# Loop projections in 64-row halves, and the feed-forward tiles turned by DMA, in a fused attention and routed-FFN kernel

## The chip, the cores and the metric

One core of one Trainium2 chip. The metric is the device time of one execution in microseconds. The kernel before takes 1410.74 us (median of three runs, 1410.70 to 1410.93).

## The reference

x is 2048 x 512 in float32. Two branches are mixed by a gate.

```python
# A: softmax attention, 32 heads of 16
qkv = (x @ wqkv).reshape(B, S, 3, 32, 16)
p = softmax(einsum("bhqd,bhkd->bhqk", q, k) * 16 ** -0.5)
a = einsum("bhqk,bhkd->bhqd", p, v) ... @ wo
# B: two tokens of 2048 are routed through a SwiGLU FFN of width 1792
r = x @ w_r
idx = argsort(-r)[:2]
y = (silu(x[idx] @ w_gate) * (x[idx] @ w_up)) @ w_down
b = x; b[idx] += y * sigmoid(r[idx])
g = sigmoid((x * gate_w).sum(-1))
out = g * a + (1 - g) * b
```

## The kernel before

**Work.** Heads are taken in pairs, each pair in two halves of 1024 queries: 32 units. A unit has 16 steps, one for each 128 keys, so there are 512 steps. A step makes S^T for two heads and two blocks of 512 queries: four S^T pieces (`s_piece`, L668), each one 50-row product into a `st` tile of PSUM and one exp on ACT into a quarter of the `P` tile of that step (L671, L677). A row of the 50 carries the negated row maximum, so that the exp needs no subtraction. The maxima of a unit are made 21 steps ahead: 64 pieces a unit (`m_piece`, L584), each one 48-row product, and DVE takes the maximum straight out of PSUM (L598): two pieces together from `mxa`, one from `mxb`. When a unit's pieces are done, `m_unit` (L644) reduces them on DVE and splits the result on POOL in two (L77, L78); `m_rows` transposes it and SP writes it into rows 48 and 49 of `Qx`. `p_v` (L940, product at L698) multiplies the `P` tile of a step with V: four column blocks of 32, accumulated over the unit in `av`.

**Two heads, two row halves.** The two heads of a pair lie in rows 0 to 63 and 64 to 127 of `Qx` and `Kx`. Pieces of S^T and of the maxima use either half (j = 0 or 1), and two that follow one another in different halves run side by side in the array. P·V, the projections and the output products use all 128 rows.

**Buffers.** PSUM has eight banks: three for `st`, two for `mxa`, one each for `mxb`, `av` and `fl`. `P` has three buffers in SBUF, `o` six, `w` (weights and later small tiles) three. The program order is written out by hand; each engine runs its own instructions in that order, and waits come from the tiles.

**The main loop** (L1000) is a string, ORDER (L31). One pass is a slot: 12 S^T pieces (s), 12 pieces for the maxima (m), three P·V (A) and one filling step (f). 164 slots cover all the maxima. At a slot's start `run_late` issues what was put off (evictions of `fl`, mostly). `at_step` hangs other work on step numbers, `gaps` hangs small DVE work behind a reduction.

**What fills.** `slots` (L882) is a generator that f advances; a yield ends a slot's share. It runs the projections of q and k for the groups 1 to 3 (`proj`, L147: 12 products of 128 rows into `fl`, three a slot, 24 projections; `evict`, L204: one copy on ACT, two instructions on POOL, stores by SP), then turns the two routed rows of x (`x_rows`), then gate and up of the FFN (`ff_in`), their transposes (`ff_t`), the down product, the sum of its four column blocks (`ff_sum`), and then the output products with wo (`wo_groups`, `wo_last`).

**The end.** The last 20 steps have no maxima left (L1025): each takes two pairs of S^T pieces and one P·V, and every second one a filling step. Then `tail` (L800) finishes the last unit.

Of the kernel before, what the change touches and what calls it, by code (L numbers as in the profile page):

```python
# [23 lines left out]
LEAD = 21  # L24
# [6 lines left out]
ORDER = "sssmmA smssmmA msssmmf smssmmAm".replace(" ", "")  # L31
# [5 lines left out]
def gated_mix(ctx: ExitStack, tc: tile.TileContext, xT, x, wqkv, wo, w_rg, w_gate, w_up, w_down,  # L37
# [60 lines left out]
    rsel = cp.tile([2, 1], F32, name="rsel")  # L98
# [5 lines left out]
    x_scr = dram.tile([S, D], F32, name="x_scr")  # L104
    i_scr = dram.tile([128, 1], U32, name="i_scr")
# [40 lines left out]

    def proj(g, which, nb, piece):  # L147
        i = "qk".index(which)
        wh, wl = W[g]
        ps = fl_tile() if g else st_tile()  # L150
        n = 0
        for terms in (((wh, xh), (wl, xh)), ((wh, xl),)):
            for c in range(4):
                for a, b in terms:
                    nc.tensor.matmul(ps, a[:, i, c, :], b[nb][:, c, :], start=n == 0, stop=n == 11)  # L155
# [194 lines left out]
    def route_rows():  # L350

        nc.vector.max_index(idx8, top8, rg["row"])
        nc.gpsimd.tensor_copy(num8, idx8)
# [41 lines left out]
    def load_down(j):  # L395
        t = xp.tile([FK, 4, D], F32, tag=f"xh{j}", name=f"wd{j}")
        nc.sync.dma_start(t, ap(w_down, j * FC * D, [[D, FK], [FK * D, 4], [1, D]]))
        ff.setdefault("down", []).append(t)

    def ff_in(name):  # L400
# [7 lines left out]
        late.append((ff_evict, (name, [128, FC], ps)))  # L408
        yield

    def ff_evict(name, shape, ps):
        ff[name] = o_tile(name, shape)
        nc.scalar.activation(ff[name], ps, AF.Copy)

    def ff_t(i, name):
        ps = fl_tile((FK, 4, 128))
        for cc in range(4):
            nc.tensor.transpose(ps[:, cc, :], ff[name][:, cc * FK:(cc + 1) * FK], ident)
        late.append((ff_gu, (i, ps)))

    def ff_gu(i, ps):
        if i == 0:
            ff["gu"] = o_tile("gu", [FK, 2, 4, 4, 2])
        nc.scalar.activation(ff["gu"][:, i], ps.rearrange("p c (j m) -> p c j m", m=32)[:, :, :, 0:2], AF.Copy)

    def ff_act():
        ff["e"] = o_tile("ffe", [FK, 4, 4, 2])
        nc.scalar.activation(ff["e"], ff["gu"][:, 0], AF.Exp, scale=-1.0)
        ff["hT"] = o_tile("ffhT", [FK, 4, 4, 32])
        nc.gpsimd.memset(ff["hT"], 0.0)  # L430
        nc.gpsimd.tensor_scalar(ff["e"], ff["e"], 1.0, None, op0=OP.add)
        nc.gpsimd.tensor_mul(ff["gu"][:, 1], ff["gu"][:, 0], ff["gu"][:, 1])

    def ff_h():
        nc.vector.reciprocal(ff["e"], ff["e"])
        nc.gpsimd.tensor_mul(ff["hT"][:, :, :, 0:2], ff["gu"][:, 1], ff["e"])

    def ff_down():
        ps = fl_tile()
        for cc in range(4):  # L440
            for j in range(4):
                nc.tensor.matmul(ps[32 * j:32 * j + 32, :], ff["hT"][:, cc, j, :], ff["down"][j][:, cc, :],  # L442
# [3 lines left out]
        late.append((ff_evict, ("y4", [128, D], ps)))  # L446
        yield

    def ff_sum():
        ps = fl_tile((2, 512))  # L450
        nc.tensor.matmul(ps, sel_j, ff["y4"], start=True, stop=True)
        late.append((ff_out, (ps,)))

    def ff_out(ps):
        y = o_tile("ffy", [2, D])
        nc.scalar.activation(y, ps, AF.Copy, scale=rsel[:, 0:1])
        nc.gpsimd.tensor_add(y, y, xsel)
        nc.gpsimd.indirect_dma_start(out=x_scr, out_offset=bass.IndirectOffsetOnAxis(ap=idx2[:, :1], axis=0),
                                     in_=y, in_offset=None)
# [5 lines left out]
    acc = []  # L465
# [10 lines left out]
    def acc_add(t, ps, scale):  # L476
# [3 lines left out]
        nc.gpsimd.tensor_add(a, a, w)  # L480
# [3 lines left out]
    def load_wo():  # L484
        s = ring.tile([128, 4, D], F32, tag="xs", name="wos", bufs=2)
        nc.sync.dma_start(s, ap(wo, 0, [[D, 128], [128 * D, 4], [1, D]]))
# [24 lines left out]
    def wo_terms(ps, ah, al, c, sl, first, last):  # L511
        for n, (a, b) in enumerate(((ah, wop[0]), (al, wop[0]), (ah, wop[1]))):
            nc.tensor.matmul(ps, a[:, sl], b[:a.shape[0], c, :], start=first and n == 0, stop=last and n == 2)  # L513
# [55 lines left out]
    def wo_last(t, k):  # L569
# [4 lines left out]
        if now[0] < STEPS - LEAD - 1:  # L574
            late.append((acc_add, (t, ps, gg)))
        else:
            finish(t, ps)
        if k == 128:
# [288 lines left out]
    at_step(26, gather)  # L867
    at_step(-8, load_w, 1)
# [13 lines left out]
    def slots():  # L882
        for w, nb in order:
            yield from proj(1, w, nb, 3)
        late.append((split_w, (2,)))
        at_step(now[0] + 4, load_w, 3)
        x_rows()
        yield
# [11 lines left out]
        ff_t(0, "gate")  # L900
        yield
        yield from ff_in("up")
        ff_t(1, "up")
        late.append((ff_act, ()))
        at_step(now[0] + 3, gaps.append, ff_h)
        at_step(now[0] + 3, load_wo)
        for c in range(4):
            at_step(now[0] + 6 + c, split_wo, c)
        at_step(now[0] + 5, load_at, 0, (0, 1))
        at_step(now[0] + 13, split_at, 0, (0, 1))  # L910
        yield
        yield
        yield from ff_down()
        ff_sum()
# [4 lines left out]
        for t in range(16):  # L919
            at_step(s + 6 + t, acc_scale, t)  # L920
        yield
# [18 lines left out]
    def p_v(s):  # L940
# [10 lines left out]
        elif u == QU - 1:  # L951
            for i in range(8):
                at_step(s + 6 + i, gaps.append, partial(l_out, 3, i))
            for i in range(4):
                at_step(s + 16 + 2 * i, l_last, i // 2, i % 2)
                at_step(s + 19 + 2 * i, n_last, i // 2, i % 2)
            at_step(s + 27, split_last, 3)
# [41 lines left out]

    while count["m"] < UNITS * EL:  # L1000
# [3 lines left out]
        for o in ORDER:  # L1004
            if o == "s":
# [3 lines left out]
                s_piece(s, i % 2, i // 2)  # L1009
# [3 lines left out]
            elif o == "m":  # L1013
# [21 lines left out]
    end_step(STEPS + 2)  # L1035
# [36 lines left out]
```

## Time and profile before

| | |
|---|---|
| median of three runs | 1410.74 us |
| the profiled execution | 1410.52 us |
| its span in the trace | 1408.4 us |
| granted TensorE clock | 0.999 |
| instructions in the trace | 24050 |
| DMA | 101.24 MB, 72 GB/s over the span |

A row of the timeline is: start in us from the span's start, length in us, engine, line, operation, what is written and read, shape, count of merged instructions, and in brackets the idle time of the engine before it and what ended it. A row of groups ends with: busy us, mean ns of one, idle us before them. A row of windows is: stretch, its length, busy us (and count) of PE, PEld (weight loads), DVE, ACT, POOL, then granted clock, DMA share, GB/s. Ends of PE's products are modelled; its starts are measured. POOL's spans are rough.

### The profile page before, as it was taken

The page shows a single profiled execution, that of the slowest core. Times are in us where ns is not written, and L with a number is a line of the kernel's source. Part 1 is how long each engine was busy: PE and PEld are TensorE (multiplying, and loading weights), DVE is VectorE, ACT ScalarE, POOL GpSimd, SP SyncE. Part 2 cuts the span into 40 slices and gives each one's busy share as a digit, 9 for nine tenths or more (in the row PEclk, how much of TensorE's full clock was granted, in tenths as well). Part 3 has the DMA queues.
Part 4 walks back from the last instruction along what each step waited for, and adds up shares of the span by engine and source line. Part 5 has one row for each costly group of instructions (what it writes and reads, how often), then busy time and mean ns, then how long its engine had stood idle before and what let it go on. Part 6 is the DMA issues. An engine that isn't in the chain of part 4 may idle for free.

```text
span 1408.4 us, 24050 instructions
## 1 busy us (share of the span) xinstructions
PE 1401.3 (99%) x9093; PEld 626.8 (45%) x9093; DVE 1289.1 (92%) x1544; ACT 1169.6 (83%) x2262; POOL 318.0 (23%) x336
## 2 busy tenths in 40 slices
PE   9999999999999999999999999999999999999998
PEld 6754444444444444444444443444444444444433
DVE  6889999999999999999999999999999999999953
ACT  5578888888888888888888888888888888888987
POOL 3841101002000001200000100043822322233421
PEclk9999999999999999999999999999999999999999
DMA  8721201313132221312222342424312121111002
GB/s 260 280 50 39 55 30 39 84 39 77 38 81 94 70 61 46 77 39 74 63 91 61 94 107 70 103 60 121 84 46 54 32 61 35 30 31 46 18 28 105
DMA packets 54775, 101.24 MB, mean 72 GB/s; under 512 B 13168, under 2 KB 20592, under 8 KB 53028
## 3 DMA queue, kind: packets, MB, share of 16 engines
q1 hardware_dynamic: 53796, 98.62, 24.6%
q8 instruction: 72, 1.18, 0.4%
q10 hardware_dynamic: 576, 0.79, 0.2%
q0 software_dynamic: 288, 0.30, 0.1%
q14 instruction: 43, 0.35, 0.1%
HBM read 63.77 MB, written 36.96 MB: 72 GB/s over the span
## 4 chain that ended last, share of the span: by engine, by line
PE 99%; DVE 0%; DMA 0%; ACT 0%; issue 0%; DVEq 0%
PE av L698 36%; PE st L675 24%; PE mxa L594 12%; PE mxb L594 10%; PE fl L155 6%; PE fl L513 4%; PE st L301 3%; PE st L155 2%; PE fl L404 1%; PE mxa L628 0%; PE mxa L675 0%; PE fl L442 0%; DMA ws<-wqkv 0%; PE st L628 0%; PE av L301 0%; PE mxb L628 0%
## 5 line engine op out<-in xcount | busy, mean ns | idle before, releaser
L677 ACT ACTIVATE P<-st 128x512 f32<-128x512 f32 x2009 | 1055.0, 599 | 186.5 <-PE st L675 97.7
L598 DVE TENSOR_REDUCE Mr<-mxa 128x2 f32<-128x1024 f32 x655 | 796.3, 1216 | 1.5 <-PE mxa L594 1.3
L698 PE MATMUL av<-P,V 128*32 128x512 f32 x4096 | 545.5, 605 | 0.2 <-DVE o L710 0.2
L675 PE MATMUL st<-Qx,Kx 50*128 50x512 f32 x2009 | 530.8, 443 | 0.2 <-ACT P L677 0.2
L598 DVE TENSOR_REDUCE Mr<-mxb 128x1 f32<-128x512 f32 x654 | 451.2, 690 | 59.7 <-PE st L675 18.8
L675 PEld LDWEIGHTS st<-Qx,Kx 50*128 50x128 f32 x2009 | 277.0, 184 | 227.0 <-ACT P L677 209.0
L594 PE MATMUL mxb<-Kx,Qx 48*128 48x512 f32 x654 | 325.2, 497 | 0.0
L594 PE MATMUL mxa<-Kx,Qx 48*128 48x512 f32 x1310 | 293.7, 417 | 0.0
L594 PEld LDWEIGHTS mxb<-Kx,Qx 48*128 48x128 f32 x654 | 119.5, 183 | 273.7 <-DVE Mr L598 272.5
L698 PEld LDWEIGHTS av<-P,V 128*32 128x32 f32 x4096 | 81.1, 108 | 142.1 <-issue 135.3
L594 PEld LDWEIGHTS mxa<-Kx,Qx 48*128 48x128 f32 x1310 | 123.1, 183 | 44.4 <-DVE Mr L598 2.3
L208 POOL TENSOR_SCALAR ev<-pe 128x512 fp32r<-128x512 f32 x24 | 35.8, 1490 | 411.4 <-ACT pe L206 411.4
L480 POOL TENSOR_TENSOR acc<-acc,w 128x512 f32<-128x512 f32 x37 | 47.3, 1281 | 200.5 <-ACT w L479 200.5
L77 POOL TENSOR_SCALAR hl<-m 128x16 fp32r<-128x16 f32 x31 | 7.8, 252 | 296.4 <-DVE m L646 296.4
L155 PE MATMUL fl<-xh,wh 128*128 128x512 f32 x96 | 42.9, 447 | 0.0
L155 PE MATMUL fl<-xh,wl 128*128 128x512 f32 x96 | 40.4, 421 | 0.0
L513 PE MATMUL fl<-woh,ahl 128*128 128x512 f32 x96 | 35.2, 447 | 0.0
L564 DVE SCALAR_TENSOR_TENSOR acc<-fl,gg,acc 128x512 f32<-128x512 f32 x11 | 8.2, 747 | 29.1 <-PE fl L513 29.1
L155 PE MATMUL fl<-xl,wh 128*128 128x512 f32 x96 | 32.6, 421 | 0.0
L209 POOL TENSOR_TENSOR ev<-pe,ev 128x512 fp32r<-128x512 f32 x24 | 30.9, 1286 | 2.0
L303 ACT ACTIVATE V<-st 128x512 f32<-128x512 f32 x15 | 9.0, 598 | 23.7 <-PE st L301 23.7
L474 POOL TENSOR_SCALAR acc<-acc,omg 128x512 f32<-128x512 f32 x16 | 24.8, 1565 | 10.5 <-DMA acc<-x_scr 10.5
(189 smaller groups left out, 789.2 us busy)
## 6 DMA issues: line engine op xcount, KB each, us to landing
Kx<-k_scr SPq DMA_DIRECT2D x30, 384.0 KB
Qx<-q_scr SPq DMA_DIRECT2D x52, 192.0 KB
q_scr<-ev SPq DMA_DIRECT2D x15, 512.0 KB
k_scr<-ev SPq DMA_DIRECT2D x13, 512.0 KB
xn<-x SPq DMA_DIRECT2D x4, 1024.0 KB
Qx<-hr SPq DMA_DIRECT2D x256, 2.0 KB
acc<-x_scr SPq DMA_DIRECT2D x4, 1024.0 KB
q_scr<-ev SPq DMA_DIRECT2D x15, 256.0 KB
```

The lines of the kernel that those rows point to most:

```text
L155: nc.tensor.matmul(ps, a[:, i, c, :], b[nb][:, c, :], start=n == 0, stop=n == 11)
L208: nc.gpsimd.tensor_scalar(ev[:, 0], t, 1.0, None, op0=OP.mult)
L209: nc.gpsimd.tensor_sub(ev[:, 1], t, ev[:, 0].bitcast(F32))
L301: nc.tensor.matmul(ps, a[nb][:, c, sl], b[:, c, :], start=c == 0 and n == 0, stop=c == 3 and n == 2)
L474: nc.gpsimd.tensor_scalar(a, a, omg[:, t:t + 1], None, op0=OP.mult)
L480: nc.gpsimd.tensor_add(a, a, w)
L513: nc.tensor.matmul(ps, a[:, sl], b[:a.shape[0], c, :], start=first and n == 0, stop=last and n == 2)
L594: nc.tensor.matmul(dst, Qx[u % 3][64 * j:64 * j + 48, t * 128:t * 128 + 128], k_of(u, t // 4)[64 * j:64 * j + 48, c * 512:c * 512 + 512], ...
L598: nc.vector.tensor_reduce(Mr[:, g0:g0 + (2 if r == 1 else 1)], MX[r - 1], axis=AX.X, op=OP.max, negate=True)
L675: nc.tensor.matmul(ps, k, q, start=True, stop=True)
L677: nc.scalar.activation(P[s][:, 2 * j + c, :], ps, AF.Exp)
L698: nc.tensor.matmul(AV[0][32 * ct:32 * ct + 32, :], V[:, kt, h * VW:h * VW + 32], P[s][:, ct, :], start=kt == 0, stop=kt == KT - 1)
```

## The change

- In slots 1 to 95 the three products of a projection's slot become six of 64 rows: h for rows 0 to 63, H for rows 64 to 127, set among the pieces of S^T and of the maxima by a new ORDER, in which a capital is a piece or half in rows 64 to 127. A half that follows one of the other rows waits, through a nop on POOL, until that one has ended, since both add into one bank.
- Slot 0 and the slots from 96 on keep the old order, written as ORDER_FF.
- In the new ORDER the second P·V of a slot stands after nine S^T pieces; before, after six.
- The routed rows of x, and gate and up, are turned by DMA instead of transposes on PE; the four blocks of the down product are added on POOL instead of PE. This takes four filling slots out.
- The last 20 steps run three pairs of S^T pieces to a turn and then the P·V that are ready, with a filling step every second turn: six output products there, ten before.
- The weight splits of groups 2 and 3 are issued at the end of the projections of the group before; the scaling of `acc` is spread over more steps; `wo` is loaded in four transfers.

```diff
-ORDER = "sssmmA smssmmA msssmmf smssmmAm".replace(" ", "")
+ORDER = "sSsmMASmShMmhhSMsHHsHsmMAmSsSMmAM"
+ORDER_FF = "sSsmMA SmsSMmA MsSsmMf SmsSMmAM".replace(" ", "")
+H_SLOTS = range(1, 96)
...
+    pend, fresh, halving = [[], []], [], [False]
+    def mm(ps, a, b, start, stop):
+        if not halving[0]:
+            nc.tensor.matmul(ps, a, b, start=start, stop=stop)
+            return
+        if start:
+            fresh.append(ps)
+        for j in range(a.shape[0] // 64):
+            pend[j].append((ps, a[64 * j:64 * j + 64], b[64 * j:64 * j + 64]))
+        last_one[0] = stop
+    def half(j):
+        if pend[j]:
+            ps, a, b = pend[j].pop(0)
+            stop = not pend[0] and not pend[1] and last_one[0]
+            i = nc.tensor.matmul(ps, a, b, start=bool(fresh), stop=stop)
+            if before[0] is not None and before[1] != j:
+                n = nc.gpsimd.nop()
+                tc.add_manual_dep(n.ins, before[0].ins.name, SYNC, reason="one bank")
+                tc.add_manual_dep(i.ins, n.ins.name, SYNC, reason="one bank")
+            before[:] = i, j
+            fresh.clear()
...
-                    nc.tensor.matmul(ps, a[:, i, c, :], b[nb][:, c, :], start=n == 0, stop=n == 11)
+                    (mm if g else nc.tensor.matmul)(ps, a[:, i, c, :], b[nb][:, c, :], start=n == 0, stop=n == 11)
...
-            if (g, which, nb) == (2, "q", 3):
-                late.append((split_w, (3, (1,))))
-                at_step(now[0] + 2, split_w, 3, (0,))
+            if g < 3 and (which, nb) == ("q", 3):
+                late.append((split_w, (g + 1, (1,))))
+                at_step(now[0] + 3, split_w, g + 1, (0,))
...
     def x_rows():
-        ps = fl_tile((128, 4, 2))
-        for c in range(4):
-            nc.tensor.transpose(ps[:, c, :], xsel[:, c * 128:c * 128 + 128], ident[:2, :2])
-        late.append((nc.scalar.activation, (xselT[:, :, 0:2], ps, AF.Copy)))
+        nc.sync.dma_start(xs_scr, xsel)
+        for m in range(2):
+            nc.sync.dma_start(xselT[:, :, m], ap(xs_scr, m * D, [[1, 128], [128, 4]]))
+        for j in range(1, 4):
+            nc.sync.dma_start(rsel4[32 * j:32 * j + 2, :], rsel)
...
+    def ff_turn(name):
+        ff_evict(name, [128, FC], ff["ps"])
+        ff["T" + name] = o_tile("T" + name, [FK, 2, 16])
+        for m in range(2):
+            nc.sync.dma_start(ff["T" + name][:, m], ff[name].rearrange("(j m) n -> j m n", m=32)[:, m, :])
...
+    def ff_y4(ps):
+        ff_evict("y4", [128, D], ps)
+        yy = ring.tile([128, 2, D], F32, tag="w", name="yy", bufs=3)
+        ff["yy"] = yy[0:2, 0], yy[0:2, 1], o_tile("y3", [128, D])[0:2]
+        for j, t in enumerate(ff["yy"]):
+            nc.sync.dma_start(t, ff["y4"][32 * j + 32:32 * j + 34, :])
...
+    slot = 0
     while count["m"] < UNITS * EL:
         hold = count["A"] % KT == 0 and count["A"] > 0
         if not hold:
             run_late()
-        for o in ORDER:
+        whole = slot not in H_SLOTS
+        halving[0] = not whole
+        asked = False
+        for o in ORDER_FF if whole else ORDER:
+            j = int(o.isupper())
...
             else:
-                next(fills, None)
+                if not asked:
+                    asked = True
+                    next(fills, None)
+                if o in "hH":
+                    half(j)
+        slot += 1
-    for s in range(count["s"] // 4, STEPS + 2):
-        run_late()
-        if s < STEPS:
-            start_step(s)
-            s_pair(s, 0)
-            s_pair(s, 1)
-        p_v(s - 2)
-        if s < STEPS and (s - count["s"] // 4) % 2 == 0:
-            next(fills, None)
-        end_step(s)
+    first, done = count["s"] // 2, count["A"]
+    for k, p in enumerate(range(first, 2 * STEPS, 3)):
+        run_late()
+        for i in range(p, min(p + 3, 2 * STEPS)):
+            s, c = divmod(i, 2)
+            if c == 0:
+                start_step(s)
+            s_pair(s, c)
+            if c:
+                end_step(s)
+        ready = (p + 1) // 2
+        for s in range(done, ready):
+            p_v(s)
+            if s == done and k % 2 == 0:
+                next(fills, None)
+        done = ready
```

More of the change, by code (lines that the diff above doesn't have):

```diff
@@ L97, in gated_mix @@
     Mr = cp.tile([128, 3 * EL], F32, name="Mr")
-    rsel = cp.tile([2, 1], F32, name="rsel")
+    rsel4 = cp.tile([128, 1], F32, name="rsel")
+    rsel = rsel4[0:2, :]
     xsel = cp.tile([2, D], F32, name="xsel")
@@ L104, in gated_mix @@
     x_scr = dram.tile([S, D], F32, name="x_scr")
+    xs_scr = dram.tile([2, D], F32, name="xs_scr")
     i_scr = dram.tile([128, 1], U32, name="i_scr")
@@ L407, in ff_in @@
                 yield
-        late.append((ff_evict, (name, [128, FC], ps)))
+        ff["ps"] = ps
+        late.append((ff_turn, (name,)))
         yield
@@ L479, in acc_add @@
         nc.scalar.activation(w, ps, AF.Copy, scale=scale[:, t:t + 1])
-        nc.gpsimd.tensor_add(a, a, w)
+        if scaled.get(t, 0) > now[0]:
+            at_step(scaled[t], nc.gpsimd.tensor_add, a, a, w)
+        else:
+            nc.gpsimd.tensor_add(a, a, w)
     wop = []
@@ L485, in load_wo @@
         s = ring.tile([128, 4, D], F32, tag="xs", name="wos", bufs=2)
-        nc.sync.dma_start(s, ap(wo, 0, [[D, 128], [128 * D, 4], [1, D]]))
+        for c in range(4):
+            nc.sync.dma_start(s[:, c], ap(wo, c * 128 * D, [[D, 128], [1, D]]))
         wop.append(xp.tile([128, 4, D], F32R, tag="xl0", name="woh"))
@@ L512, in wo_terms @@
         for n, (a, b) in enumerate(((ah, wop[0]), (al, wop[0]), (ah, wop[1]))):
-            nc.tensor.matmul(ps, a[:, sl], b[:a.shape[0], c, :], start=first and n == 0, stop=last and n == 2)
+            mm(ps, a[:, sl], b[:a.shape[0], c, :], start=first and n == 0, stop=last and n == 2)
     def wo_part(t, gs):
@@ L867, in gated_mix @@
     at_step(26, gather)
+    at_step(36, x_rows)
     at_step(-8, load_w, 1)
@@ L953, in p_v @@
                 at_step(s + 6 + i, gaps.append, partial(l_out, 3, i))
[L954 to L957, printed above, removed]
+            for n, i in enumerate((3, 0, 1, 2)):
+                at_step(s + 15 + 2 * n, l_last, i // 2, i % 2)
+                at_step(s + 17 + 2 * n, n_last, i // 2, i % 2)
+            at_step(s + 18, split_last, 3)
         elif QU <= u < UNITS - 1:
```

103 lines of the change are left out of this document (50 added, 53 removed).

## The prediction

> **What bounds the kernel now.** I read the page first (engine shares, costliest groups), then the timeline of one stretch of the loop, slot by slot, then a slot with no filling work, then the windows of the end.
>
> ```profile
> span 1408.4 us, 24050 instructions
> PE 1401.3 (99%) x9093; PEld 626.8 (45%) x9093; DVE 1289.1 (92%) x1544; ACT 1169.6 (83%) x2262; POOL 318.0 (23%) x336
> ...
> L677 ACT ACTIVATE P<-st 128x512 f32<-128x512 f32 x2009 | 1055.0, 599 | 186.5 <-PE st L675 97.7
> L598 DVE TENSOR_REDUCE Mr<-mxa 128x2 f32<-128x1024 f32 x655 | 796.3, 1216 | 1.5 <-PE mxa L594 1.3
> L598 DVE TENSOR_REDUCE Mr<-mxb 128x1 f32<-128x512 f32 x654 | 451.2, 690 | 59.7 <-PE st L675 18.8
> ```
>
> PE is never idle by the page, yet DVE is 92% busy with two kinds of reduction, 1216 and 690 ns, and the two engines hand one buffer `mxa` and one buffer `mxb` to and fro. So I look at one passage of a slot (12 S^T pieces, 12 pieces for the maxima, three P·V, one filling burst `fl`).
>
> ```profile
> 300.31 0.46 PE L594 MATMUL mxa<-Kx,Qx 48*128 48x512 f32 x2
> ...
> 300.70 0.96 PE L155 MATMUL fl<-xl,wh 128*128 128x512 f32 x3
> ...
> 301.59 0.50 PE L594 MATMUL mxb<-Kx,Qx 48*128 48x512 f32 x1
> ...
> 302.17 0.51 PE L594 MATMUL mxa<-Kx,Qx 48*128 48x512 f32 x2
> ...
> 303.57 0.62 ACT L206 ACTIVATE pe<-fl 128x512 f32<-128x512 f32 x1
> 303.60 0.50 PE L594 MATMUL mxb<-Kx,Qx 48*128 48x512 f32 x1
> ...
> 304.17 0.40 PE L594 MATMUL mxa<-Kx,Qx 48*128 48x512 f32 x2
> 304.28 1.49 POOL L208 TENSOR_SCALAR ev<-pe 128x512 fp32r<-128x512 f32 x1 [20.66 <-ACT pe L206]
> ...
> 304.50 1.06 PE L698 MATMUL av<-P,V 128*32 128x512 f32 x8
> 304.74 1.22 DVE L598 TENSOR_REDUCE Mr<-mxa 128x2 f32<-128x1024 f32 x1
> 305.50 0.50 PE L594 MATMUL mxb<-Kx,Qx 48*128 48x512 f32 x1
> ...
> 305.83 0.46 PE L675 MATMUL st<-Qx,Kx 50*128 50x512 f32 x2
> 305.85 1.29 POOL L209 TENSOR_TENSOR ev<-pe,ev 128x512 fp32r<-128x512 f32 x1
> ...
> 306.08 0.45 PE L594 MATMUL mxa<-Kx,Qx 48*128 48x512 f32 x2
> ...
> 306.67 1.22 DVE L598 TENSOR_REDUCE Mr<-mxa 128x2 f32<-128x1024 f32 x1
> ...
> 308.37 0.50 PE L155 MATMUL fl<-xh,wh 128*128 128x512 f32 x1
> ```
>
> A slot is 7.67 us from burst to burst (300.70 to 308.37). Four `mxa` pairs divide it into four groups. With P·V in a group: pair at 304.17, P·V at 304.50, `mxb` at 305.50, next pair at 306.08, so 1.91. With the burst: 300.31 to 302.17, 1.86. Is the burst on the path? A slot that has none answers.
>
> ```profile
> 914.41 1.22 DVE L598 TENSOR_REDUCE Mr<-mxa 128x2 f32<-128x1024 f32 x1
> ...
> 922.15 1.22 DVE L598 TENSOR_REDUCE Mr<-mxa 128x2 f32<-128x1024 f32 x1
> ```
>
> ```profile
> 917.70 3.04 ACT L677 ACTIVATE P<-st 128x512 f32<-128x512 f32 x6 [0.33 <-PE st L675]
> 917.71 0.44 PE L594 MATMUL mxa<-Kx,Qx 48*128 48x512 f32 x2
> ...
> 918.28 1.22 DVE L598 TENSOR_REDUCE Mr<-mxa 128x2 f32<-128x1024 f32 x1
> ...
> 918.35 0.49 PE L675 MATMUL st<-Qx,Kx 50*128 50x512 f32 x1 [0.20 <-ACT P L677]
> ...
> 919.55 0.52 PE L594 MATMUL mxa<-Kx,Qx 48*128 48x512 f32 x2
> ...
> 920.12 1.23 DVE L598 TENSOR_REDUCE Mr<-mxa 128x2 f32<-128x1024 f32 x1
> ```
>
> Between these first and fifth `mxa` reductions no `fl` product runs, and the slot still takes 7.74. In its burstless group PE waits, for the exps (918.35) and then for the reduction of 918.28, which ends at 919.50 and lets the next pair go at 919.55. So three groups are as long as PE makes them with P·V, and the fourth is as long as DVE's turn of `mxa`. I take 7.70 for a slot.
>
> **The halves themselves.** In 95 slots three 128-row products become six of 64 rows. The burst holds PE from 300.70 to 301.59, 0.89; half a pair costs what a pair does, 0.25 (305.83 to 306.08). The new group without P·V is the one from the second `mxa` pair to the third: one half alone, half with S, M with s, one half alone, two halves with s, then the pair, 7 intervals, 1.75. I put time 0 at the slot's first `mxb` piece (303.60). Up to the second pair nothing of PE's order changes in kind: +2.48. PE alone would set the third pair at +4.23, but the reduction of 306.67 ends at 307.89, +4.29, so DVE sets it at +4.34, its second piece up to 0.1 later (in 919.55's pair: 0.52 for both, 0.40 for one). From there as now: P·V 0.33 later, `mxb` 1.00 on, fourth pair 0.58 on, next slot's `mxb` 1.33 on: +7.58 to +7.68. Alone the halves would be worth 7.63 - 7.70 = -0.07 a slot, -7 us for 95. Bounds: 0, and -21 if the burstless group fell to PE's own 1.75 and the others kept 1.91 (7.48 a slot).
>
> By the Trainium skill, page "TensorEngine Tiling (Array Packing)", Tiling Modes, "Changing tiling mode (not just tile) drains the TensorE"; the switches that this change takes out would then be worth up to the whole burst beyond three pairs. The burst row agrees that there is a price, the empty slot says that the slot does not pay it.
>
> **The moved P·V.** This I price highest. Now the second P·V of a slot follows the sixth S^T piece; in the new order it follows the ninth (count the s and S before the second A). The ninth opens a new step, so a fourth `P` tile, and `P` has 3 buffers, unchanged. The oldest is still to be read by that very P·V. So the ninth exp waits on ACT for the P·V behind it, and exps 10 to 12 queue behind it; `st` has 3 buffers too, so the twelfth S^T piece waits on PE for the ninth exp, and the fourth `mxa` pair, the last P·V and all else on PE stand behind that.
>
> ```profile
> 132.77 1.06 PE L698 MATMUL av<-P,V 128*32 128x512 f32 x8
> ...
> 133.90 0.60 ACT L716 ACTIVATE o<-av 128x512 f32<-128x512 f32 x1
> ```
>
> ACT goes 0.07 after the end of a P·V (133.83 to 133.90). P·V starts at +4.67 to +4.77, ends 1.06 later, the ninth exp runs from +5.80 to +5.90 for 0.60, the twelfth piece goes 0.05 after it (first of six exps 917.70 plus 0.60, PE at 918.35), at +6.45 to +6.55 in place of about +6.05. Fourth pair 0.25 later, next slot 1.33 after that: +8.03 to +8.13. I take 8.08: 0.38 over 7.70, 95 times, **+36 us**, the -7 in it. Bounds: 7.9 (the reduction starts as soon as in 919.55 to 920.12, and no late second piece) gives +19, 8.15 gives +43.
>
> **The relay through POOL.** Two halves of one bank are kept apart by a nop on POOL between h and H. The trace holds no nop. Its lower bound is the moment when POOL has handed out all that stands before it, its upper the end of that work; I take the lower plus 0.1, since the nop has nothing to compute and needs no result of POOL's. In an ordinary slot nothing stands before it: the third h goes at +2.98, lasts 0.40, and H at +3.48 is hardly held. But L208 and L209 (evict) and the splits of `hl` stand before it.
>
> ```profile
> L208 POOL TENSOR_SCALAR ev<-pe 128x512 fp32r<-128x512 f32 x23 | 34.3, 1490 | 392.8 <-ACT pe L206 392.8
> ...
> L77 POOL TENSOR_SCALAR hl<-m 128x16 fp32r<-128x16 f32 x18 | 4.5, 252 | 194.9 <-DVE m L646 194.9
> ```
>
> ```profile
> 198.06 0.47 PE L594 MATMUL mxa<-Kx,Qx 48*128 48x512 f32 x2
> ...
> 198.63 1.22 DVE L598 TENSOR_REDUCE Mr<-mxa 128x2 f32<-128x1024 f32 x1
> ...
> 200.52 0.22 POOL L78 TENSOR_TENSOR hl<-m,hl 128x16 fp32r<-128x16 f32 x1
> ```
>
> ```profile
> 159.26 0.45 PE L675 MATMUL st<-Qx,Kx 50*128 50x512 f32 x2
> ...
> 159.92 0.22 POOL L78 TENSOR_TENSOR hl<-m,hl 128x16 fp32r<-128x16 f32 x1
> ```
>
> Evict, 23 times: the first h is due with the S of 305.83; L209 is handed out at 305.85 when L208 is done: 0.1 each, 2.5. Unit ends, 18 in the loop's halved part, each third of them at another `mxa` pair of the slot (64 pieces a unit, 12 a slot). At the first pair: h due at 159.26, POOL past L78 at 159.92, so 0.75 late, six times, 4.5. At the second: H due four intervals after 198.06, 199.06; POOL past L78 at 200.52, so H at 200.6, the third pair 0.75 later at 201.37 where DVE allows 199.90: 1.45, six times, 8.7. At the third: the next half is a slot away, 0. The second part of the weight split now falls just before an H, twice: behind L209's end (307.14) one 1.49 op, H at 308.7 where 307.1 was due, 3. Early routing on POOL, 2: an estimate, four short waits for DVE or ACT of about one 0.5 step. Together **+21**. Bounds 0 and 54 (all POOL work to its end: 307.14 for 305.85, 23 times, and L78's 0.22).
>
> The Trainium skill, page "PSUM — Partial Sum Buffer", Engine vs sequencer instructions, says the sequencer only waits for prior instructions "to be *dispatched* to the engine, not to complete", which is the lower bound; by the other reading the sum would be 1498. No run here shows it yet.
>
> **FF by DMA, four slots less.** Removed: 12 transposes, the sum product, four ACT copies; added: some 13 small transfers on SP's queue, `wo` in four, a few POOL ops. PE's part was filling, and filling is free (7.74 empty, 7.67 full): 0. What hides it is DVE's turn of `mxa`; were that gone a burst would cost its 0.89. Each turned tile has a slot (7.7) until its first reader; On SP the reads of `xs_scr` wait for its write, and a turn waits for ACT's copy; behind them stand loads that are issued a unit ahead of their use. Bounds -2 and +3.
>
> **The end.**
>
> ```profile
> 1351.00:1397.00 46.00, 45.80 (x296) 15.40 (x297) 11.54 (x18) 41.89 (x72) 1.76 (x3) 1.00 0.17 59
> ```
>
> PE fills the 46 us, ACT 41.89 of them. Four bursts fewer and three pairs to a turn let ACT become the limit: at most -4, I take **-2**; +2 if a P·V comes to wait for its exps.
>
> **Sum.** The profiled execution took 1410.52 us with a span of 1408.4; the median of three runs is 1410.74. 1410.5 + 36 + 21 + 0 - 2 = 1465.5; I say **1465**.
>
> **Rivals.**
> (1) POOL relays only after its work has ended: 1465 + 33 = 1498. For it: h and H are PE's, the nop is in POOL's order. Against: it reads nothing of POOL's. 10%.
> (2) The ninth exp does not hold PE, some piece of slack covers it: 1465 - 43 = 1422. Against: `P` and `st` both have three buffers in the code, and the twelfth piece has 0.4 too little. 12%.
> (3) Faster. One mechanism: PE's switches between whole and halved array are what sets the slot, in the burst's group and through late second pieces in the next. It decides wherever the new slot comes under 7.70. With 7.48 (the bound above) and no hold: 1410.5 - 21 - 2 = 1387. For it: PE 99% busy, DVE's `mxb` reductions idle 59.7 us in all. Against: the empty slot. 13%. By the tiling rule of the Trainium skill alone it would be the first guess.
> (4) The halves do not run beside S and M at all: four intervals more a slot, 95 of 1.0 us, 1560. Against: pieces in the trace start together in pairs. 2%.
> (5) Gains and holds cancel, about 1410: 3%.
> The forecast: 60%; its own range is 1438 to 1482 (+19 for +36, -10 on POOL; +7, +10).
>
> **How the numbers follow.** Range 1416 to 1498: the forecast's whole range, (2) and most of (1); (3), (4), (5) and some tails are left out. Slower by over 0.2% (about what this measurement can tell from none): 60 + 10 + 12 + 2 = 84%; within it 3%; faster 13%.
>
> **What would show it.** Right: in slots 1 to 95 the ninth exp starts 0.07 after the slot's second P·V, the twelfth `st` piece waits for ACT, slot 8.0 to 8.1; later slots stay 7.70. PE waits for POOL at six unit ends by about 0.75 and at six by 1.5; hardly at evictions. The third `mxa` pair goes 0.05 after DVE's reduction. Wrong: slots under 7.70, a ninth exp that does not wait, or waits for POOL at all 23 evictions over a microsecond (then rival 1).

## The result, and the profile after

The changed kernel takes **1497.6 us** (median of 6 runs, 1493.8 to 1506.1) against 1410.8 before: a ratio of **1.063, 95% interval 1.0605 to 1.065**. (One of the six runs of before took 1601.2 us; it is a slow run and not in the ratio.) The forecast was 1465; the result stands at the very end of its range, 1498. The direction and the two mechanisms named were there; two more were not foreseen.

The profiled execution took 1506.1 us, 95.6 more than that of before; it is the slowest of the six, so what is counted below in its trace adds up to more than the medians differ by. First the page of the kernel after: span, busy time of the engines, the granted clock in 40 slices, the three groups shown of before, and the halves.

```profile
span 1504.3 us, 24935 instructions
...
PE 1466.9 (98%) x9364; PEld 633.5 (42%) x9364; DVE 1297.0 (86%) x1540; ACT 1165.9 (77%) x2262; POOL 327.9 (22%) x348
...
PEclk9999999998999899999989998999999999999999
...
L726 ACT ACTIVATE P<-st 128x512 f32<-128x512 f32 x2009 | 1050.8, 601 | 285.4 <-PE av L747 94.2
L647 DVE TENSOR_REDUCE Mr<-mxa 128x2 f32<-128x1024 f32 x655 | 797.6, 1218 | 55.3 <-PE mxa L643 50.1
...
L647 DVE TENSOR_REDUCE Mr<-mxb 128x1 f32<-128x512 f32 x654 | 450.1, 688 | 91.1 <-PE st L724 42.7
...
L170 PE MATMUL fl<-xh,wh 64*128 64x512 f32 x188 | 76.3, 406 | 7.7 <-POOLq L173 7.7
```

There are as many exps and reductions as before, each as long as before. The idle time has changed: ACT's exps now wait for P·V (`av`), 94 us in all, where the waits of before hold no such wait, and the clock row has 8s where before it was all 9s. The loss lies in slots 1 to 95. Their first and last `mxa` reductions (timeline of DVE), after and before:

```profile
97.06 1.21 DVE L647 TENSOR_REDUCE Mr<-mxa 128x2 f32<-128x1024 f32 x1
...
926.71 1.21 DVE L647 TENSOR_REDUCE Mr<-mxa 128x2 f32<-128x1024 f32 x1
```

```profile
96.29 1.21 DVE L598 TENSOR_REDUCE Mr<-mxa 128x2 f32<-128x1024 f32 x1
...
829.52 1.21 DVE L598 TENSOR_REDUCE Mr<-mxa 128x2 f32<-128x1024 f32 x1
```

829.65 us in place of 733.23, so +96.4; from there to the end of the span 577.6 in place of 578.9, so -1.3. The median of the 95 slots is 8.28 (7.71 before): 95 x 0.57 = **54**. The other **42** stand in some 25 single slots. An ordinary slot first, from PE's timeline (start, duration, count) and ACT's:

```profile
138.94 0.49 PE L643 MATMUL mxb<-Kx,Qx 48*128 48x512 f32 x1
...
143.28 0.49 PE L643 MATMUL mxa<-Kx,Qx 48*128 48x512 f32 x2
143.71 1.07 PE L747 MATMUL av<-P,V 128*32 128x512 f32 x8
144.70 0.49 PE L643 MATMUL mxb<-Kx,Qx 48*128 48x512 f32 x1
144.71 1.34 PE L724 MATMUL st<-Qx,Kx 50*128 50x512 f32 x3
145.56 0.73 PE L643 MATMUL mxa<-Kx,Qx 48*128 48x512 f32 x2
146.21 1.06 PE L747 MATMUL av<-P,V 128*32 128x512 f32 x8
147.21 0.49 PE L643 MATMUL mxb<-Kx,Qx 48*128 48x512 f32 x1
```

```profile
141.37 2.59 ACT L726 ACTIVATE P<-st 128x512 f32<-128x512 f32 x5 [0.22 <-PE mxb L643]
144.90 2.07 ACT L726 ACTIVATE P<-st 128x512 f32<-128x512 f32 x4 [0.94 <-PE av L747]
```

8.27 from `mxb` to `mxb`. The second P·V ends at 144.78, and at 144.90 the ninth exp starts, which had waited 0.94 for it; the twelfth S^T piece, last of the three at 144.71, must wait for that exp, and with it the `mxa` pair at 145.56. This is the forecast's chain, link by link. Now one of the slots that stand out, slot 30, from the timelines of PE and POOL:

```profile
346.53 0.50 PE L724 MATMUL st<-Qx,Kx 50*128 50x512 f32 x1
348.31 0.50 PE L170 MATMUL fl<-xh,wh 64*128 64x512 f32 x1 [1.28 <-POOLq L173]
...
349.44 1.93 PE L747 MATMUL av<-P,V 128*32 128x512 f32 x8
```

```profile
347.95 0.25 POOL L81 TENSOR_SCALAR hl<-m 128x16 fp32r<-128x16 f32 x1 [17.98 <-DVE m L695]
348.28 0.22 POOL L82 TENSOR_TENSOR hl<-m,hl 128x16 fp32r<-128x16 f32 x1
```

The first H half waits for the relay's nop, which stands behind L82 on POOL, and goes 0.03 after L82 has *begun*: the lower of the forecast's two readings of the nop. (The Trainium skill, "PSUM — Partial Sum Buffer", Engine vs sequencer instructions, has a nop wait for dispatch only; this row agrees.) But the P·V behind takes 1.93 for eight products in place of 1.06. The windows of the kernel after, cut within 0.1 us of the places where the granted clock changes (length; busy time and count of PE, PEld, DVE, ACT, POOL; clock; DMA), say why:

```profile
345.95:349.36 3.41, 2.13 (x15) 1.12 (x12) 2.47 (x4) 2.14 (x5) 0.47 (x2) 1.00 0.00 0
349.36:352.77 3.41, 3.41 (x15) 1.20 (x14) 1.97 (x3) 1.55 (x4) 0.00 (x0) 0.51 0.00 1
352.77:356.19 3.42, 3.42 (x17) 1.03 (x14) 1.48 (x3) 1.14 (x3) 0.00 (x0) 0.50 0.02 3
356.19:359.60 3.41, 3.41 (x16) 1.03 (x14) 1.85 (x3) 1.58 (x4) 0.00 (x0) 0.50 0.01 1
359.60:363.01 3.41, 3.41 (x26) 1.67 (x23) 3.31 (x4) 2.50 (x5) 2.22 (x2) 0.99 0.00 0
```

After the wait TensorE runs at half clock for 10.24 us: 15 to 17 products in 3.41 us where the next window has 26. There are seven stretches at half clock in the loop, of 3.41 or 10.24 us, 51 us together; the loop of before has none. Five follow second-pair unit ends like this one (slots 30, 46, 62, 78, 94). The other two, behind slots 16 and 64, follow a wait that the forecast doesn't have either: the waits of PE and PEld between 96 and 930 us (total, times, longest) hold it, beside the two that were foreseen.

```profile
ACT P L726 <- PE av L747: 94.2, 94, 2.2
...
PEld fl L170 <- POOLq L173: 18.0, 20, 1.9
...
PE fl L170 <- POOLq L173: 11.2, 13, 1.6
...
PE av L747 <- ACT o L776: 6.5, 5, 1.3
```

In slots 16, 32, 48, 64 and 80 a unit ends with the second P·V of a slot. ACT then copies `av` in two halves, the second (L776) three S^T pieces later, as it did before. That second half now stands behind the held exps, and the next unit's first P·V waits 1.3 for it.

So the 42 us are made up of these parts: six first-pair unit ends at +0.74 (4.4), six second-pair at about +1.35, taken from slot 14, which has no half clock behind it (8.1), slot 1 with the early routing (1.7), five waits for the copy at +1.36 (6.8); the other **21** stand in the slots with the stretches at half clock and behind them, 0.42 lost for each of the 51 us.

### The profile page after: what moved, and what is told of

Read it like the earlier page. It is cut to its first block, busy times and chain, and to the rows that moved or that the text cites. A ratio compares the mean times of both kernels' runs of the same rounds, so it can differ in the third digit from the quotient of the medians.

```text
span 1504.3 us, 24935 instructions
## 1 busy us (share of the span) xinstructions
PE 1466.9 (98%) x9364; PEld 633.5 (42%) x9364; DVE 1297.0 (86%) x1540; ACT 1165.9 (77%) x2262; POOL 327.9 (22%) x348
## 4 chain that ended last, share of the span: by engine, by line
PE 89%; ACT 5%; DVE 2%; DMA 2%; issue 1%; SPq 0%; POOL 0%; ACTq 0%; DVEq 0%; POOLq 0%
PE av L747 35%; PE st L724 20%; PE mxa L643 11%; PE mxb L643 9%; PE fl L170 6%; ACT P L726 4%; PE fl L158 4%; PE st L336 3%; DVE Mr L647 2%; DMA xs<-xT 1%; DMA wvs<-wqkv 1%; PE fl L442 0%; DMA q_scr<-ev 0%; PE mxa L677 0%; PE mxa L724 0%
## 5 line engine op out<-in xcount | busy, mean ns | idle before, releaser
L724 PE MATMUL st<-Qx,Kx 50*128 50x512 f32 x2009 | 654.7, 453 | 11.4 <-ACT P L726 1.4
L747 PE MATMUL av<-P,V 128*32 128x512 f32 x4096 | 558.8, 618 | 7.3 <-ACT o L776 6.5
L724 PEld LDWEIGHTS st<-Qx,Kx 50*128 50x128 f32 x2009 | 292.3, 187 | 251.0 <-ACT P L726 230.2
L643 PE MATMUL mxa<-Kx,Qx 48*128 48x512 f32 x1310 | 326.2, 428 | 0.0
L170 PE MATMUL fl<-xh,wh 64*128 64x512 f32 x188 | 76.3, 406 | 7.7 <-POOLq L173 7.7
L170 PE MATMUL fl<-xh,wl 64*128 64x512 f32 x190 | 76.6, 403 | 3.5 <-POOLq L173 3.5
L170 PE MATMUL fl<-xl,wh 64*128 64x512 f32 x192 | 65.6, 401 | 0.0
L170 PEld LDWEIGHTS fl<-xh,wh 64*128 64x128 f32 x188 | 34.9, 185 | 15.7 <-POOLq L173 9.6
L170 PEld LDWEIGHTS fl<-xh,wl 64*128 64x128 f32 x190 | 35.3, 186 | 11.4 <-POOLq L173 8.2
L170 PEld LDWEIGHTS fl<-xl,wh 64*128 64x128 f32 x192 | 34.5, 189 | 6.4 <-POOLq L173 0.2
```

The lines of the kernel that those rows point to most:

```text
L170: i = nc.tensor.matmul(ps, a, b, start=bool(fresh), stop=stop)
L643: nc.tensor.matmul(dst, Qx[u % 3][64 * j:64 * j + 48, t * 128:t * 128 + 128], k_of(u, t // 4)[64 * j:64 * j + 48, c * 512:c * 512 + 512], ...
L724: nc.tensor.matmul(ps, k, q, start=True, stop=True)
L747: nc.tensor.matmul(AV[0][32 * ct:32 * ct + 32, :], V[:, kt, h * VW:h * VW + 32], P[s][:, ct, :], start=kt == 0, stop=kt == KT - 1)
```

## The experiments

The theory after reading the trace (A): the slot is long because the ninth exp waits for the `P` buffer that the late second P·V still reads; the rest is the relay, the copy, and the clock behind both. Times are medians; each kernel ran beside the kernel before, which took 1410.6 to 1410.8 in each set. The last three columns come from each kernel's one profiled execution: the median slot of 1 to 95, "others" (what the 95 slots take over 95 ordinary ones) and the time at half clock.

| kernel | us | ratio, 95% | ordinary slot | others | half clock in the loop |
|---|---|---|---|---|---|
| before | 1410.8 | | 7.71 | 0.9 | 0 |
| after | 1497.6 | 1.0605–1.065 | 8.28 | 43 | 51 |
| av_back | 1526.6 | 1.080–1.083 | 8.64 | 32 | 38 |
| late_av_whole | 1549.0 | 1.096–1.100 | 9.09 | 9 | 3 |
| relay_fix | 1478.7 | 1.047–1.050 | 8.28 | 14 | 10 |
| both | 1505.4 | 1.065–1.069 | 8.64 | 7 | 7 |
| spaced | 1419.5 | 1.005–1.008 | 7.71 | 10.5 | 0 |
| spaced2 | 1434.1 | 1.0155–1.018 | 7.72 | 23.5 | 7 |
| no_halves | 1409.9 | 0.9986–1.0004 | 7.71 | 0.9 | 0 |
| relay_av | 1466.5 | 1.038–1.041 | 8.28 | 2.3 | 0 |
| spaced_av | 1413.6 | 1.001–1.003 | 7.71 | 4.0 | 0 |
| other_p | 1414.6 | 1.001–1.004 | 7.73 | 3.8 | 3 |

**av_back: the second P·V ahead of the ninth piece again.**

```
-ORDER = "sSsmMASmShMmhhSMsHHsHsmMAmSsSMmAM"
+ORDER = "sSsmMASmShMmhhSMsHHsHmMAmSsSsMmAM"
```

> One thing is undone: in slots 1 to 95 the second P.V product is issued behind the eighth S^T piece instead of behind the ninth, so that the ninth exponential waits again for a product a whole pair earlier; the halves, their pairs, the relay on POOL and everything else stay as in the kernel after. Theory A (three P buffers: the ninth exponential can't start before the second P.V of the slot has ended, and what stands behind it on ACT and then PE sets the slot): the wait of ACT for the P.V product goes (88 us in 89 waits in the kernel after), the normal slot of 1 to 95 falls from 8.27 to 7.6 to 7.8 us, and the time to 1425 to 1445 us, since the 12 unit ends with the relay's wait (12.5 us) and the stretches at half clock behind them (15 to 28 us) stay. Rival B (pairs of a half beside a piece of S^T or of the maxima are themselves slow, the wait of ACT only shows it): the slot stays at 8.2 to 8.3 us and the time at 1490 to 1500 us.

Both were wrong: 8.64, longer than after. ACT's timeline of one slot, and PE's, show what took the wait's place:

```profile
862.10 2.60 ACT L726 ACTIVATE P<-st 128x512 f32<-128x512 f32 x5 [0.16 <-PE mxb L643]
866.01 2.06 ACT L726 ACTIVATE P<-st 128x512 f32<-128x512 f32 x4 [1.30 <-PE st L724]
```

```profile
863.24 0.50 PE L724 MATMUL st<-Qx,Kx 50*128 50x512 f32 x1
...
864.44 1.06 PE L747 MATMUL av<-P,V 128*32 128x512 f32 x8
865.44 0.49 PE L643 MATMUL mxb<-Kx,Qx 48*128 48x512 f32 x1
865.44 0.73 PE L724 MATMUL st<-Qx,Kx 50*128 50x512 f32 x3
866.66 0.50 PE L724 MATMUL st<-Qx,Kx 50*128 50x512 f32 x1 [0.48 <-ACT P L726]
```

No exp waits for P·V any more, but the eighth piece is issued at 863.24 and the ninth at 865.44: two halves, a pair for the maxima and P·V stand between, 2.2 us without an S^T piece. ACT runs dry for 1.30; then three pieces come at once, fill `st`, and PE waits 0.48 for ACT. Theory A alone falls; what follows is theory C: any stretch in which ACT gets no piece, or may not start one, comes back as PE's wait for a free `st` buffer, because PE can be only three pieces ahead.

**late_av_whole: the late P·V without halves.**

```
-ORDER = "sSsmMASmShMmhhSMsHHsHsmMAmSsSMmAM"
+ORDER = "sSsmMASmSMmfSMsssmMAmSsSMmAM"
-        halving[0] = not whole
+        halving[0] = False
```

> The other part alone: in slots 1 to 95 the second P.V product stays where the kernel after has it, behind the ninth S^T piece, but the projections are whole products of 128 rows again, in the places of the order of before; no half, no relay on POOL. Theory A (the place of the second P.V alone makes the slot long): slots 1 to 95 at 8.1 to 8.4 us against 7.70 to 7.72 in the kernel before, no waits of PE for POOL, and no stretch at half clock behind second-pair unit ends (at most those behind a wait for ACT's copy of av); 1455 to 1480 us. Rival B (halves make it long): slots at 7.7 us, 1405 to 1415 us.

Theory A has the direction right and the size far too small: 9.09 a slot, 1.38 over before. Two rows of the waits between 96 and 880 us:

```profile
PEld st L724 <- ACT P L726: 226.6, 341, 1.7
...
ACT P L726 <- PE av L747: 79.7, 85, 1.2
```

The wait for P·V is there without any half, and PE's weights for S^T wait for ACT nearly twice as often as after (341 times; 182 there in the same stretch). The size comes from a second hold: in the slot around 300 us ACT gets no piece for 0.76 while PE runs the whole burst (300.01, 0.97 long), and the third S^T piece behind it waits 0.45 for ACT (302.09). So the halves as such aren't the loss; in this place of P·V the kernel with them is shorter by 0.81 a slot.

**relay_fix: the relay issued early.** The nop is issued behind the last H of a slot, and the maxima of a second-pair unit end are finished at the next pair:

```
+            if relay[0] is not None and j == 0:
+                tc.add_manual_dep(i.ins, relay[0].ins.name, SYNC, reason="one bank")
+                relay[0] = None
+                before[:] = None, 0
...
+            if j == 1 and not pend[1]:
+                relay[0] = nc.gpsimd.nop()
+                tc.add_manual_dep(relay[0].ins, i.ins.name, SYNC, reason="one bank")
...
-            if e == EL - 1 and r == 2 and u < UNITS - 1:
-                due.append(u)
-            elif e == EL - 1 or (e == 0 and r == 1 and g):
-                m_unit(u if e else u - 1)
+            if e == EL - 1 and r == 2 and u < UNITS - 1 or e == 0 and r == 1 and g:
+                due.append(u if e else u - 1)
+            elif e == EL - 1:
+                m_unit(u)
```

> The order of the kernel after with its halves, but the instruction on POOL that relays between the last half of one row group and the first of the other is issued right behind the last half of the slot instead of ahead of the half that waits for it, and the maxima of a unit whose last pair is the second of a slot are finished at the next pair, so that POOL's splits of them come behind the relay and not ahead of it. Theory A: the waits of PE for POOL (16 us for weights and 10 us for products in the kernel after) go to under 4 us, the second-pair unit ends fall from 9.6 to 12.7 us a slot to 8.3 to 8.6, the stretches at half clock behind them go (51 us at half in the kernel after, at most 14 left, behind the waits for ACT's copy of av), while the normal slot stays at 8.27: 1462 to 1478 us. Rival B (the half clock comes from the halves' load as such and not from waits): the half-clock stretches stay at 40 to 50 us and the time above 1482 us.

19 us less than after, 0.7 above the upper end of A's span. PE's and PEld's waits for POOL fall to 1.6 and 2.4 us (from 11.2 and 18.0), all twelve unit ends of these kinds are ordinary slots, and the five stretches at half clock behind them are gone. Three of 3.41 us stand behind slots 16, 32 and 64, where the copy of `av` is waited for.

**both: av_back and relay_fix together.**

> The second P.V product behind the eighth S^T piece again, and the relay on POOL issued behind the last half of the slot with the maxima of second-pair unit ends finished a pair later; halves kept. Theory A (late P.V, relay and the clock behind the relay's waits are the whole of the loss): slots 1 to 95 at 7.6 to 7.75 us, no stretch at half clock in the loop or one at most, 1400 to 1416 us. Rival B (halves cost something of their own, in mode switches or in the pairs): slots above 7.85 us and 1425 us or more.

A's numbers fail by the slot of av_back (8.64). B's numbers come in, but its cause, a price of the halves themselves, is what the next runs exclude.

**spaced and spaced2: the halves with the S^T pieces spread.** On relay_fix, the orders

```
+ORDER = "smMAmSSsMmAMsSsmMAmShSMmShhsMsHHH"     (spaced)
+ORDER = "sAmMSsSmAMmsSsMAmMShhhSSmsHHMmHsM"     (spaced2)
```

> The halves and the mended relay are kept and the order of slots 1 to 95 is written anew: one S^T piece, P.V, three pieces, P.V, three pieces, P.V, five pieces, with the halves among the last five, so that no exponential waits for a P.V product and no stretch of PE without an S^T piece is longer than two exponentials of 0.49 us. Theory C (formed after the P.V product put back ahead of the ninth piece gave 8.64 us a slot: it is the supply of ACT that counts, three st buffers ahead at most, and any stretch in which ACT gets no piece or may not start one comes back a moment later as PE's wait for a free st buffer): slots 1 to 95 at 7.63 to 7.75 us, as long as DVE's own 4 x (1.22 + 0.69) = 7.64, and 1398 to 1412 us. Rival B (halves have a price of their own, in pairs or switches): slots at 8.0 us or more, 1435 us or more.

> As the run before, with another order by the same rule: S^T piece, P.V, three pieces, P.V, three pieces, P.V, and the halves in other places among the last five, three of them in a row with one piece beside. Theory C: slots 1 to 95 at 7.63 to 7.80, 1398 to 1418 us. Rival D (it is not the spacing but some particular pair or place that made the slots long, and the order of the run before had it right by luck, or not): over 8.0 us a slot here.

The ordinary slot is 7.71 and 7.72: the halves add nothing to it, and with three pieces between P·V products ACT is fed. Both times are above the forecast spans, because of single slots. In spaced they are 16, 32, 48, 64 and 80 (+1.57 each, the copy of `av` again, since only three pieces lie between the P·V that ends a unit and the next), 1 and 95 (+0.8, +1.0). In spaced2 the same five hold 11 us, with half clock behind two of them, and in twelve more (3, 19 and so on to 83, and 14, 30 and so on to 94) PE waits for the relay again, 0.9 a slot: there the nop stands behind POOL's splits once more. But the ordinary slot is no shorter than before. Windows of the same 200 us, spaced and before, columns as above:

```profile
500.00:700.00 200.00, 198.50 (x1394) 89.67 (x1388) 187.98 (x214) 164.53 (x321) 24.01 (x24) 1.00 0.23 63
```

```profile
500.00:700.00 200.00, 200.00 (x1322) 87.38 (x1318) 189.93 (x218) 168.39 (x323) 24.50 (x27) 1.00 0.24 63
```

DVE is busy for 94 and 95% of them. The group without P·V, in spaced:

```profile
516.53 0.69 DVE L654 TENSOR_REDUCE Mr<-mxb 128x1 f32<-128x512 f32 x1
517.14 1.22 DVE L654 TENSOR_REDUCE Mr<-mxa 128x2 f32<-128x1024 f32 x1
518.27 0.68 DVE L654 TENSOR_REDUCE Mr<-mxb 128x1 f32<-128x512 f32 x1
518.96 1.22 DVE L654 TENSOR_REDUCE Mr<-mxa 128x2 f32<-128x1024 f32 x1
```

DVE goes from one reduction to the next without a gap, and the group lasts 1.82 (517.14 to 518.96), not much less than the three groups with P·V (medians 1.90 to 2.02). PE's freed time lies in the one group whose length DVE sets.

**no_halves: the rest of the change alone** (`H_SLOTS = range(0)`).

> The halves and their order are left out: all slots have whole products and the order of before; the turn of gate and up by DMA, the four slots less and the six products in the tail stay. Theory A: the rest of the change takes 1.3 us off the end and nothing elsewhere, slots at 7.70 to 7.72: 1408 to 1410.5 us. Rival: the transfers of the turn or the weights' smaller loads delay something in the loop that the halved kernel's slower slots hide: over 1412 us.

1409.85, the interval holds no change: the turn by DMA, the slots and the tail together are worth 0.7 us by the medians, and 2 us at the most by the interval.

**pauses: a probe of the clock** (one execution). On no_halves, a chain of writes on POOL ahead of a slot's first S^T piece:

```
+    def pause(k):
+        for n in range(k):
+            hold_for[0] = nc.gpsimd.memset(scratch, 0.0)
+            if n == 0:
+                tc.add_manual_dep(hold_for[0].ins, last_m[0].ins.name, SYNC, reason="pause")
```

> A probe on the kernel without halves: ahead of the first S^T piece of 18 slots, five slots apart, PE is made to wait for a chain of one to six writes of POOL to a spare tile (about 0.4 us each, begun when the last piece of the slot before has ended), each length three times; nothing else changes. Theory C (a wait of PE alone of some 1.3 us or more takes the granted clock to 0.5 for 3.4 or 10.2 us): no dip after the waits of up to 0.9 us, dips at 0.5 after most of those from 1.4 us on, each beginning within some us of the wait. Rival E (the half clock in the kernel after comes from the load or the kind of the halved products, not from waits): no dip here after any wait of up to 2.5 us.

| PE's wait, us | 0.54 | 1.01 | 1.49 | 1.96 | 2.44 | 2.91 | 3.4 to 4.4 |
|---|---|---|---|---|---|---|---|
| times | 1 | 2 | 1 | 3 | 3 | 3 | 5 |
| followed by half clock | 0 | 0 | 0 | 3 | 2 | 3 | 5 |

(Five came out longer than set, since POOL had an eviction to do first.) This kernel has whole products alone, and its clock halves after waits: rival E falls. But the length of the wait does not decide by itself: a wait of 2.44 passed. All stretches in the loop last 3.41 or 6.83 us here and begin on one grid of 3.413 us. Windows cut on that grid, of the wait of 2.44 that passed (first two) and of one of 2.91:

```profile
503.48:506.89 3.41, 2.35 (x15) 0.83 (x15) 2.87 (x4) 1.92 (x5) 0.88 (x3) 1.00 1.19 377
506.89:510.30 3.41, 2.04 (x15) 0.78 (x16) 1.02 (x1) 1.50 (x3) 1.20 (x3) 1.00 0.16 45
...
588.82:592.23 3.41, 1.57 (x13) 0.64 (x13) 0.55 (x1) 1.03 (x3) 1.61 (x4) 1.00 0.01 2
592.23:595.64 3.41, 3.41 (x18) 1.03 (x14) 2.48 (x3) 2.71 (x6) 0.00 (x0) 0.50 0.07 15
```

The wait that passed was split over two windows, 2.35 and 2.04 busy. So what counts here is PE's busy time in one window of the grid, or something close to it. In all windows of this run's loop at full clock, 1.98 us or less was followed by half clock and 2.04 or more was not.

**relay_av: the copy of `av` in one piece**, on relay_fix.

```
-        elif STEPS - LEAD > u * KT + KT + 2 and u % 3 == 2:
+        elif False:
```

> The kernel with the mended relay, and ACT copies av at every unit end in one piece as soon as the unit's last P.V has ended, also at the third of the unit ends at which it was copied in two halves, the second three S^T pieces later. Theory (in slots 16, 32, 48, 64 and 80 the second half of the copy stands on ACT behind the exponentials that the late second P.V holds, and the next unit's first P.V waits for it; 1.35 us a slot and the half clock behind them are the 12 us by which the relay's kernel exceeds 95 slots of 8.28): these slots fall from 9.6 to 11.0 to 8.3 us, no stretch at half clock in the loop, 1464 to 1468 us. Rival (the copy in one piece delays the exponentials by as much): slots 16 to 80 stay above 9.3 us, 1474 to 1479 us.

As the theory says: 12 us less, no stretch at half clock in the loop, and the slots other than the ordinary ones add 2.3 us, 1.7 of it in slot 1. What is left over before is the ordinary slot, 95 x 0.57 = 54.

**other_p: the same order without the wait**, on relay_av.

```
-            nc.tensor.matmul(AV[0][32 * ct:32 * ct + 32, :], V[:, kt, h * VW:h * VW + 32], P[s][:, ct, :],
+            p = P[s + 1 if s % 3 == 2 and not now[0] < 3 and now[0] < 288 else s]
+            nc.tensor.matmul(AV[0][32 * ct:32 * ct + 32, :], V[:, kt, h * VW:h * VW + 32], p[:, ct, :],
```

> The order, the halves, the mended relay and the copy in one piece as in the first run of this call, but the second P.V of each slot reads the P tile of the next step (written long before) in place of its own, so that the tile that the ninth exponential needs has no reader left and is free at once; P.V of every third step is thus left out. Every instruction and its place in its engine's order stay. Theory A (the ninth exponential's wait for the buffer that the second P.V reads is what makes the slot long): slots 1 to 95 fall from 8.28 to 7.65 to 7.80 us, 1408 to 1420 us. Rival (the wait only shows that ACT is late, or the pairs themselves are slow): slots stay at 8.2 or more, 1464 to 1468 us.

The second P·V of a slot now reads the tile of the next step, which is already written, so this kernel leaves out the P·V of every third step; no instruction changes its place. 52 us go, the slot is 7.73. ACT's timeline of one slot:

```profile
502.90 3.10 ACT L733 ACTIVATE P<-st 128x512 f32<-128x512 f32 x6 [0.29 <-PE mxb L650]
506.80 1.57 ACT L733 ACTIVATE P<-st 128x512 f32<-128x512 f32 x3 [0.81 <-PE st L731]
```

Six exps in a row, the ninth among them, where after had five and a wait of 0.94. With the same order on every engine, the buffer is the whole of the long slot.

**spaced_av: the copy in one piece, on spaced.**

> The first re-spaced order (1419.5 us), with the copy of av in one piece as in the run before. Theory C: the slots 16, 32, 48, 64 and 80 fall from 9.28 to 7.7 to 7.9 us, and the time to 1410.5 to 1413 us, no better than the kernel before, since slots stay at 7.70, DVE's turn of the maxima, however little PE does. Rival (with the last holds gone PE's freed time shows): slots under 7.66 and under 1407 us.

Theory C again, a little over its span: slots 32 and 64 still hold 0.7 each, 1 and 95 as in spaced. No slot is under 7.66. No version tried is faster than the kernel before by more than the noise.

## Why the prediction was right or wrong

The three steps from after to before, each by one experiment: relay and the clock behind it 19 us (relay_fix), the copy of `av` and the clock behind that 12 (relay_av), the ninth exp's wait 52 (other_p); 3.8 are left, 3.1 of it in slot 1, which has a stretch at half clock in the profiled execution.

**The bound: right.** The forecast had three groups set by PE with P·V and one by DVE, and so took the burst's removal as nearly free. spaced shows it, and refutes rival (3): with well-placed halves the slot is 7.71, not 7.48; a price of the halves that fits into DVE's group would not show. Even the -0.07 a slot that the walk allowed did not show.

**The moved P·V: mechanism right, term mis-sized.** 8.08 forecast, 8.28 measured, so 54 for 36. P·V starts at +4.77, the upper end of the forecast, and the exp 0.12 after its end, not 0.07: the twelfth piece goes at +6.62 (with 145.56), 0.12 later than the 6.50 in the middle of the forecast. And the `mxa` pair is done only a step of 0.34 later, that of the first pieces after a stop, where I took the 0.25 of running pairs: 0.09. other_p confirms the cause; rival (2), that slack covers it, is out. What the step did not see is that the place of P·V is only one way to starve ACT: av_back would have been my remedy, and lost 29 us more.

**The relay: right.** The nop waits for dispatch alone, so rival (1) is out, and that its 1498 is nearly the measured time is chance. Rival (4) is out as well, since spaced runs the halves in slots of 7.71. The delays measured are 0.74 for 0.75 and 1.35 for 1.45; the evictions and the weight splits, 5.5 in the sum, show as nothing or 0.3 here and there: 14 for 21.

**FF by DMA, the end: right.** 0 and -2 forecast; -1.3 in the profile, no change that can be told in no_halves.

**The failed step** is the unit end. "At the second: H due four intervals after 198.06 ... 1.45, six times, 8.7" counted the delay and stopped there. The wait leaves PE idle 1.28 of a 3.41 us window, and half clock follows for up to 10.24 us: 21 us in the profiled run. And of the held exps I followed only what is behind them on PE, not the half copy of `av` on ACT's own queue: 6.8 us, and two of the seven stretches. relay_fix and relay_av, which take these waits away, take the stretches away with them. By terms of the profiled execution: slots +18, relay -7, copy +7, clock +21, end +1, together the 40 between 1465.5 and 1506.1.

## What to carry to other kernels

When a product moves in an order written by hand, follow the buffers that it releases to every engine that writes them, and then everything that stands behind the held instruction on its own queue. Where one engine feeds another through a few buffers, count the longest stretch without a feeding piece: moving the stall elsewhere in the same order made it larger, spreading the pieces removed it. And before buying PE time, see which group of the loop would get it: here it went to the group that DVE sets, so the best order gave nothing.

## What the hardware showed beyond the expected

**A short stop of TensorE halves its clock, by windows.** The stretches last one, two or three times 3.41 us and begin on one grid in each run. In the probe a window with PE busy 1.98 us or less of 3.41 was followed by half clock. After has a window with 2.13 busy that was (345.95, above) and this one that wasn't:

```profile
209.53:212.94 3.41, 2.12 (x17) 0.83 (x15) 2.28 (x4) 1.60 (x3) 0.47 (x2) 1.00 0.00 0
212.94:216.35 3.41, 3.29 (x24) 1.23 (x20) 2.75 (x5) 2.29 (x5) 0.00 (x0) 1.00 0.01 2
```

so busy time is near the measure but not the measure itself, with the limit at about 2.0 to 2.1 of 3.41 us. The Trainium skill, page "TensorE: Matmul & The Clock Gate", Part 1, gives a free-running window of 3413 ns and two states; the traces agree. It has the clock fall after a window without work, of about 3.4 us; here 1.28 us of idle time was enough when it fell into one window, and the measurement decides. Since the grid does not start with the program (the stretches begin 1.27 us past a multiple of 3.413 from the span's start in after, 1.72 in pauses), the same wait brings no half clock in slot 14, and some 4 us more in slots 30 and 31. It also fits the spread of after's six runs, 12 us, against 2 us over the four of relay_av, whose profiled execution has no half clock in the loop: the mean granted clock of the six is 0.983 in the two slowest (1506.1 and 1505.4) and rises to 0.991 in the fastest (1493.8), in the order of their times. Why some stretches last one window and others three stays open.

**The first step after a stop or a P·V is slower:** the next piece follows 0.33 to 0.34 after the first ones there (S^T pieces at 144.71 and 145.04), 0.23 to 0.25 in a running row of pairs.
